# Fourth unit of a chunked RWKV6 and SiLU-MLP kernel: bonus products and a weight difference put elsewhere in the order, two quarter products exchanged

## The chip, the cores and the metric

The kernel runs on one core of one Trainium2 chip. The metric is the time on the device in microseconds (us); lower is better. Three timed runs of the kernel before gave 632.41, 632.80 and 632.97 us, median 632.8 us.

The engines are called as in the profile: PE is the matmul engine (PEld its weight loads), DVE the vector engine, ACT the scalar engine, POOL GpSimd, SP the engine that here only issues DMAs. A "q" behind a name is the engine's sequencer, where it waits for semaphores or issues DMAs.

## The reference

Two blocks follow each other. The first is a linear attention with a decay of its own for each channel (batch 4, 8 heads, 768 tokens, head size 48), the second a two-layer MLP with SiLU on the 3072 tokens (384 channels, 2048 hidden):

```python
for t in range(S):
    cur = np.einsum('bhd,bhe->bhde', u[None] * kt, vt)      # bonus of the token itself
    y[:, :, t] = np.einsum('bhd,bhde->bhe', rt, state + cur)
    state = wt[:, :, :, None] * state + np.einsum('bhd,bhe->bhde', kt, vt)
...
h = x @ w_in                                                # x: 3072 x 384
g = h * (1.0 / (1.0 + np.exp(-h)))
return (g @ w_out).astype(np.float32)
```

## The kernel before, in words

**Units.** The work is cut into 12 units, numbered 0 to 11: each is 128 tokens of two batches, 256 tokens in all. Units 0 to 2 are written out step by step together with the rounding of the weights; from unit 3, the fourth, a loop takes over. The change touches unit 3 and, in one point, every unit's output products.

**Attention of one unit.** The 128 tokens of a chunk see each other through a 128x128 matrix `score`, built in levels l = 0 to 6: at level l, blocks of 2^l tokens are paired. Before level l can be multiplied, the keys `tk` must have been grown by decays (`grow_keys`, L625, POOL, two instructions for each level, with `odd_keys`, L595, ACT, that copies the odd blocks ahead of it) and the queries `tr` too (`grow_queries`, L607, DVE). `prepare(l)` does the same and writes the grown queries into a second buffer (L737 on DVE, L739 on ACT), so that `burst(l)` can multiply levels l and l+1 one right after the other (L669, PE; first into `p_sc`, then into `p_m`). `keep_level` copies a level's result under a mask into `score` (L679, DVE). `product` (L408, POOL) makes the decays `tw` of the next level.

**The bonus.** The diagonal of `score` is a product of its own. For units below 4, `bonus(0)`, `bonus(1)` and `bonus(2)` (L428, L430, L432, all POOL) multiply r, k and u into the buffer `ruk`; `bonus_sum(0)` (L437) and `bonus_sum(1)` (L441, twice) reduce it on DVE. Both `bonus(0)` and `bonus(1)` write the first half of the same buffer, so `bonus(1)` waits for `bonus_sum(0)`. `bonus_sum(1)` ends with four small DMAs on SP (`diag<-own_sums`, L447); `bonus_spread` (L575 and L577 on ACT, L578 on DVE) and `bonus_write` (L584, DVE) put the sums on the diagonal. `load_rk` (L139) and `load_u` (L259) load the next unit's r, k, w and u for the bonus; `make_block_mask` (L478 on POOL, L480 to L483 on DVE) makes a mask that units from 4 on use.

**MLP of one unit.** `up(m)`, m = 0 to 7, multiplies `w_in` (L929, PE) into `p_h`, two buffers, which ACT turns into `gt` (L938). The output product is done with seven quarter products in place of eight (a Strassen-like scheme): `quarter(which)`, which = 0 to 6, each of 8 accumulated matmuls (L995, PE) into `p_o`, two buffers, and then one or two additions on DVE (L1004) that empty it. The products need sums of `gt` quarters, called s1 to s4 here and held in `temps` (`sums`, L977, DVE), and differences of weight quarters t1, t2, t3 in the buffer `own` (`weight_sums`, L969, DVE, 128x1536 each). `weight_sums(2)` makes t3 = b22 - b12; `weight_sums(3)` then overwrites b12.

**Order.** Within an engine, instructions run in the order in which the program writes them. `mix(i)` lists the steps of unit i in groups. Behind each group the loop puts some of the MLP steps of the two units before: `downs(i - 2)`, the seven quarters of unit i - 2, then `ups(i - 1)`, the eight ups of unit i - 1. For unit 3 the counts are

```python
room = (1, 1, 0, 2, 1, 1, 1, 1, 1, 2, 2, 1, 1, 0) if i < NPAIR else (3, 2, 2, 1, 1, 1, 2, 1, 1, 1, 0)
for group, count in zip(groups, room):
    do(*group)
    for step in steps[:count]:
```

so quarters 0 and 1 come behind groups 0 and 1, quarters 2 and 3 behind group 3, quarters 4, 5 and 6 behind groups 4, 5 and 6, then up 0 behind group 7, up 1 behind group 8, ups 2 and 3 behind group 9, and ups 4 and 5 behind group 10. `burst(1)` opens group 4, `burst(3)` group 7 and `burst(5)` group 10. On PE, unit 3 therefore reads: quarters 0 to 3, burst 1, quarters 4 to 6, burst 3, ups 0 to 3, burst 5, ups 4 to 7 with the rest of the attention between them.

## Time and profile before

| what | value |
|---|---|
| timed runs, median (lowest to highest) | 632.8 us (632.41 to 632.97) |
| the profiled execution's own time | 632.14 us |
| its span, first to last instruction | 630.4 us |
| PE busy | 621.7 us, 99% of the span |
| PEld busy | 563.5 us, 89% |
| DVE / POOL / ACT busy | 434.8 (69%) / 364.5 (58%) / 187.2 us (30%) |
| TensorE clock granted, mean over the span | 0.997 of full speed |
| unit 3 on PE, quarter 0 to the end of burst 5 | 127.53 to 167.17 us |

The span is the time from the first to the last instruction of one profiled execution; its own time, 632.14 us, is what the clock of the timed runs would show for it. The times in the trace count from the span's start. A busy PE is not PE at its peak: a matmul at half clock is busy for longer, so the granted clock has to be read beside the busy time.

### The profile page before, as it was taken

The numbers are of one execution on the slowest core, as the hardware profiler recorded it, in microseconds if no ns is written. First come the engines' busy times: TensorE is split into PE (matmuls) and PEld (weight loads), VectorE is DVE, ScalarE is ACT, GpSimd is POOL, SyncE is SP. The second block draws the span as 40 slices with busy tenths as digits, with TensorE's granted clock in tenths as the row PEclk, the third lists the DMA queues.
The fourth block names the chain that finished last, engine by engine and source line by source line (L and its number), as shares of the span: only waits on it lengthen the run. The fifth ranks groups of instructions, "written<-read, shape, count | busy, mean of one in ns | idle before, by whom it ended". The sixth has DMA issues, their size and how long they took to land.

```text
span 630.4 us, 12322 instructions
## 1 busy us (share of the span) xinstructions
PE 621.7 (99%) x4606; PEld 563.5 (89%) x4606; DVE 434.8 (69%) x749; ACT 187.2 (30%) x380; POOL 364.5 (58%) x414
## 2 busy tenths in 40 slices
PE   8999999998999999999999999999999999999997
PEld 7888876897899899899899899889989989989997
DVE  7879779898695694794595586587497586561041
ACT  6798891220320320320321221221221121120110
POOL 6998298566666567577478378368468458400000
PEclk9999999998999999999999999999999999999999
DMA  9966964443534543543543543452453212100000
GB/s 229 289 177 139 191 173 50 90 78 64 109 61 70 103 65 68 102 64 58 110 63 52 120 60 53 105 75 51 99 85 52 67 43 52 34 1 27 25 1 25
DMA packets 203067, 53.25 MB, mean 84 GB/s; under 512 B 186752, under 2 KB 194816, under 8 KB 203008
## 3 DMA queue, kind: packets, MB, share of 16 engines
q1 hardware_dynamic: 201424, 51.88, 40.8%
q10 hardware_dynamic: 1584, 0.59, 0.4%
q8 instruction: 36, 0.59, 0.4%
q14 instruction: 23, 0.19, 0.1%
HBM read 43.21 MB, written 5.24 MB: 77 GB/s over the span
## 4 chain that ended last, share of the span: by engine, by line
PE 92%; DVE 3%; POOL 2%; ACT 1%; DMA 1%; issue 1%; SPq 0%; POOLq 0%; DVEq 0%; ACTq 0%
PE p_h L929 40%; PE p_o L995 31%; PE p_sc L669 5%; PE p_m L951 3%; PE p_m L807 3%; PE p_m L669 3%; PE p_m L794 3%; PE p_m L781 1%; PE p_sc L821 1%; DMA raw<-in_r_dram 1%; POOL tk L625 1%; PE p_m L845 0%; DVE score L584 0%; DVE tr L607 0%; POOL w_in_sb L241 0%
## 5 line engine op out<-in xcount | busy, mean ns | idle before, releaser
L929 PE MATMUL p_h<-xt,w_in_sb 128*128 128x256 f32 x1152 | 259.0, 382 | 0.7 <-POOL tk L649 0.7
L929 PEld LDWEIGHTS p_h<-xt,w_in_sb 128*128 128x128 f32 x1152 | 216.6, 191 | 33.0 <-POOL tk L649 0.9
L938 ACT ACTIVATE gt<-p_h 128x512 f32<-128x512 f32 x90 | 53.7, 597 | 266.2 <-PE p_h L929 266.1
L625 POOL TENSOR_TENSOR tk<-tk,tw 128x256 f32<-128x256 f32 x128 | 87.3, 702 | 71.9 <-ACT tk L595 41.2
L995 PE MATMUL p_o<-own,temps 128*128 128x192 f32 x528 | 88.1, 326 | 0.4 <-DVE temps L1004 0.4
L995 PE MATMUL p_o<-w_out_sb,gt 128*128 128x192 f32 x508 | 87.4, 328 | 0.0
L995 PEld LDWEIGHTS p_o<-own,temps 128*128 128x128 f32 x528 | 86.0, 190 | 0.8 <-DVE temps L1004 0.7
L995 PEld LDWEIGHTS p_o<-w_out_sb,gt 128*128 128x128 f32 x508 | 82.7, 190 | 0.9 <-issue 0.4
L487 POOL TENSOR_TENSOR ruk<-tokens_rk 128x768 f32<-128x768 f32 (+1 forms) x32 | 51.4, 1616 | 38.7 <-DMA tokens_rk<-in_k_dram 26.1
L408 POOL TENSOR_TENSOR tw<-tw 128x256 f32<-128x256 f32 (+6 forms) x83 | 44.0, 530 | 44.6 <-DVE tw L360 40.7
L977 DVE TENSOR_TENSOR temps<-gt 128x256 f32<-128x256 f32 x84 | 52.8, 629 | 19.0 <-ACT gt L938 19.0
L679 DVE COPY_PREDICATED score<-mask,p_sc 128x512 f32<-128x512 int8 x62 | 44.5, 772 | 15.3 <-PE p_sc L669 14.7
L607 DVE TENSOR_TENSOR tr<-tr,tw 128x512 f32<-128x512 f32 x61 | 47.5, 779 | 3.7 <-POOL tk L625 1.0
L595 ACT COPY tk<-tk 128x256 f32<-128x256 f32 x52 | 21.0, 403 | 81.7 <-POOL tk L625 67.8
L669 PEld LDWEIGHTS p_sc<-tr,tk 48*128 48x128 f32 x512 | 31.4, 187 | 10.3 <-issue 7.6
L669 PE MATMUL p_sc<-tr,tk 48*128 48x128 f32 x512 | 37.7, 285 | 0.6 <-POOL tk L625 0.6
L1004 DVE TENSOR_TENSOR partial<-p_o,partial 128x192 f32<-128x192 f32 x33 | 11.7, 354 | 28.4 <-PE p_o L995 28.4
L1004 DVE TENSOR_TENSOR temps<-p_o,partial 128x192 f32<-128x192 f32 x22 | 7.8, 357 | 33.2 <-PE p_o L995 22.4
L995 PE MATMUL p_o<-w_out_sb,temps 128*128 128x192 f32 x176 | 30.4, 326 | 0.0
L1004 DVE TENSOR_TENSOR ob<-p_o,partial 128x192 f32<-128x192 f32 x22 | 7.8, 357 | 32.4 <-PE p_o L995 32.4
L995 PEld LDWEIGHTS p_o<-w_out_sb,temps 128*128 128x128 f32 x176 | 28.9, 190 | 0.0
L487 POOL TENSOR_TENSOR tokens_rk<-tokens_rk,tokens_w 128x192 f32<-128x192 f32 (+1 forms) x32 | 27.5, 878 | 1.3
(170 smaller groups left out, 845.2 us busy)
## 6 DMA issues: line engine op xcount, KB each, us to landing
w_out_sb<-in_moe_w_in_dram SPq DMA_DIRECT2D x6, 768.0 KB, 7.0
w_out_sb<-in_moe_w_out_dram SPq DMA_DIRECT2D x4, 768.0 KB, 5.5
own<-in_moe_w_out_dram SPq DMA_DIRECT2D x4, 768.0 KB, 5.3
tokens_rk<-in_r_dram SPq DMA_DIRECT2D x8, 384.0 KB, 4.6
tokens_rk<-in_k_dram SPq DMA_DIRECT2D x8, 384.0 KB, 5.6
tokens_w<-in_w_dram SPq DMA_DIRECT2D x8, 384.0 KB, 6.6
xt<-yt SPq DMA_DIRECT2D x60, 48.0 KB, 2.0
raw<-in_w_dram SPq DMA_DIRECT2D x80, 32.0 KB, 2.5
```

Source lines behind the costliest of these rows:

```text
L408: engine.tensor_tensor(out=up, in0=t[:, :, 0::2], in1=t[:, :, 1::2], op=ALU.mult)
L487: mul = lambda out, one, two: nc.gpsimd.tensor_tensor(out=out, in0=one, in1=two, op=ALU.mult)
L595: nc.scalar.copy(out=keys(i, X[(l + 1) % 2] * L + c, [4 * c, blocks], [c, 2], [1, c]), in_=keys(i, NP * L + c, [4 * c, blocks], [NP * L + ...
L607: nc.vector.tensor_tensor(out=odd, in0=odd, in1=tw[i][l][:, :, 0::2][:, :, :, None].to_broadcast([128, Q, L >> (l + 1), c]), op=ALU.mult)
L625: nc.gpsimd.tensor_tensor(out=out, in0=have, in1=odd_products(i, l, b, *blocks), op=ALU.mult)
L669: nc.tensor.matmul(bass.AP(tensor=s_p.tensor, offset=s_p.offset, ap=[s_p.ap[0], [apart * L // 2, 2], [1, L // 2]]), lhsT=tk[i][rows, X[l % ...
L679: nc.vector.copy_predicated(out=dst, mask=masks[l][:, :, None].to_broadcast([128, NB, NP, ni, c]), data=sc[e].rearrange("p (b q) (i c) -> ...
L929: nc.tensor.matmul(p_h[:, a, :], lhsT=w_in_sb[:, c, f * 128:(f + 1) * 128], rhs=xt[i][:, c, :], start=(c == 0), stop=(c == KC - 1))
L938: nc.scalar.activation(out=gt[i, m], in_=p_h, func=AF.Silu)
L977: nc.vector.tensor_tensor(out=out, in0=one, in1=two, op=op)
L995: nc.tensor.matmul(p, lhsT=left(f), rhs=right[:, f, :], start=(f == 0), stop=(f == FH - 1))
L1004: nc.vector.tensor_tensor(out=to, in0=p, in1=known, op=ALU.add)
```

## The change

For unit 3, `bonus(0)` moves from group 4 to group 6, behind `prepare(3)`, which grows the keys of level 3. `bonus_sum(0)`, `bonus(1)` and `bonus(2)` move from group 5 to group 7, behind `burst(3)` and its first `keep_level`. `bonus_sum(1)`, `load_rk` and `load_u` move from group 7 to group 8, and `make_block_mask` from group 8 to group 9.

For all units, quarters 3 and 4 change places: quarter 3 is now s1 times t1, quarter 4 is s3 times t3. The additions behind them follow: quarter 3 has one, quarter 4 two, as before.

`weight_sums(2)`, which makes t3, moves from the end of the steps written out for unit 2 into group 2 of unit 3, behind `prepare_keys(1)`. `weight_sums(3)` keeps its place, right behind `burst(1)` in group 4.

No instruction is added or removed on any engine. On PE and ACT the order of instructions is the same as before, but for the operands of the two exchanged quarters; on SP too. On POOL and DVE the moved steps stand elsewhere.

```diff
-                      [(burst, i, 1), (keep_level, i, 1), (bonus, i, 0)],
-                      [(keep_level, i, 2), (go_on, i, 2), (bonus_sum, i, 0), (bonus, i, 1), (bonus, i, 2)],
-                      [(prepare, i, 3), (reverse_v, i)],
-                      [(burst, i, 3), (keep_level, i, 3), (bonus_sum, i, 1), (load_rk, i + 1), (load_u,)],
-                      [(keep_level, i, 4), (go_on, i, 4), (make_block_mask,)],
-                      [(prepare, i, 5), (bonus_spread, i), (bonus_write, i)],
+                      [(burst, i, 1), (keep_level, i, 1)],
+                      [(keep_level, i, 2), (go_on, i, 2)],
+                      [(prepare, i, 3), (reverse_v, i), (bonus, i, 0)],
+                      [(burst, i, 3), (keep_level, i, 3), (bonus_sum, i, 0), (bonus, i, 1), (bonus, i, 2)],
+                      [(keep_level, i, 4), (go_on, i, 4), (bonus_sum, i, 1), (load_rk, i + 1), (load_u,)],
+                      [(prepare, i, 5), (make_block_mask,), (bonus_spread, i), (bonus_write, i)],
...
-        left, right = ((g(0, 0), b11), (g(0, 1), b21), (s(1), t2), (s(2), t3), (s(0), t1), (g(1, 1), b12), (s(3), b22))[which]
+        left, right = ((g(0, 0), b11), (g(0, 1), b21), (s(1), t2), (s(0), t1), (s(2), t3), (g(1, 1), b12), (s(3), b22))[which]
...
-        for to, known in ((), ((c11, u1),), ((u2, u1),), ((u3, u2),), ((c22, u3), (u4, u2)), ((c21, u3),), ((c12, u4),))[which]:
+        for to, known in ((), ((c11, u1),), ((u2, u1),), ((u4, u2),), ((u3, u2), (c22, u4)), ((c21, u3),), ((c12, u4),))[which]:
...
-       (load_values, 3), *both(turn_k, 2), (weight_sums, 2), (up, 1, 7), (sums, 1, 2))
+       (load_values, 3), *both(turn_k, 2), (up, 1, 7), (sums, 1, 2))
...
         if i == NTOK + 1:
 
+            groups[2].append((weight_sums, 2))
             groups[4].insert(1, (weight_sums, 3))
```

## The prediction

> **What bounds the kernel now.** I read the busy shares and the chain of waits first, then the timeline of PE around unit 3, then what PE waited for there, and last the granted clock of that stretch. The page says that PE is the bound:

> ```profile
> PE 621.7 (99%) x4606; PEld 563.5 (89%) x4606; DVE 434.8 (69%) x749; ACT 187.2 (30%) x380; POOL 364.5 (58%) x414
> ...
> PE 92%; DVE 3%; POOL 2%; ACT 1%; DMA 1%; issue 1%; SPq 0%; POOLq 0%; DVEq 0%; ACTq 0%
> ```

> Only what PE idles, or does at less than full clock, can be won. The timeline of PE (start, duration, instruction, in brackets the idle time ahead and its releaser) shows unit 3 and then the same stage of unit 4:

> ```profile
> 132.83 2.76 PE L995 MATMUL p_o<-own,temps 128*128 128x192 f32 x16
> 135.98 2.87 PE L995 MATMUL p_o<-own,temps 128*128 128x192 f32 x16 [0.38 <-DVE temps L1004]
> ...
> 148.77 1.16 PE L669 MATMUL p_sc<-tr,tk 48*128 48x128 f32 x16
> 151.92 1.86 PE L669 MATMUL p_m<-tr,tk 48*128 48x128 f32 x16 [1.98 <-POOL tk L625]
> 153.71 11.55 PE L929 MATMUL p_h<-xt,w_in_sb 128*128 128x256 f32 x48
> ...
> 201.39 1.16 PE L669 MATMUL p_sc<-tr,tk 48*128 48x128 f32 x16
> 202.38 1.06 PE L669 MATMUL p_m<-tr,tk 48*128 48x128 f32 x16
> 203.38 13.22 PE L929 MATMUL p_h<-xt,w_in_sb 128*128 128x256 f32 x60
> ```

> In unit 4 the two halves of a burst start 0.99 apart; in unit 3 the second half of burst 3 starts 3.15 after the first, held by keys from POOL. POOL's own timeline says why:

> ```profile
> 146.64 1.81 POOL L430 TENSOR_TENSOR ruk<-tokens_rk 128x768 f32<-128x768 f32 x1 [1.31 <-DVE own_sums L437]
> 148.53 2.14 POOL L432 TENSOR_TENSOR ruk<-ruk,u_bc 128x768 f32<-128x768 f32 x1
> 150.63 2.52 POOL L625 TENSOR_TENSOR tk<-tk,tw 128x256 f32<-128x256 f32 x4
> ```

> The keys of level 3 (the first two of the four L625) stand behind both bonus products. The chain of waits passes just there, DVE's L437 to L430 to L432 to L625 to PE. Last, the table of stretches (length, busy of PE, PEld, DVE, ACT, POOL, then the granted clock, DMA share and rate):

> ```profile
> 150.00:152.00 2.00, 0.08 (x2) 0.09 (x2) 2.00 (x4) 0.00 (x0) 1.92 (x4) 1.00 0.48 55
> 152.00:154.00 2.00, 2.00 (x17) 1.78 (x18) 0.37 (x2) 0.00 (x0) 1.42 (x3) 0.55 0.60 153
> 154.00:156.00 2.00, 2.00 (x6) 1.61 (x6) 1.94 (x5) 0.00 (x0) 0.00 (x0) 0.60 0.27 82
> 156.00:158.00 2.00, 2.00 (x11) 1.74 (x11) 1.08 (x3) 0.47 (x1) 0.00 (x0) 1.00 0.32 40
> ```

> PE counts as fully busy from 152 to 156, at 0.55 and 0.60 of its clock. The idle time is paid twice.

> [...]2.00 x 0.45 + 2.00 x 0.40 = 1.70 us lost, so 3.4 us at half rate[...] L969 took 2.58 us at 124.45 beside POOL's L826 and 1.75 at best.

> **The change, part by part.**

> *Bonus products behind the keys.* I compare with unit 4. There quarters 2 to 4 start at 188.30 and quarter 5 at 196.10, so 2.60 a quarter; a half burst is 0.99 to 1.00; five ups take 216.52 - 203.38 = 13.14, so 2.63 an up. Unit 3 from quarter 0 (127.53) to burst 5 (165.19) has 7 quarters, 2 bursts and 4 ups: 18.39 (quarter 0 to burst in unit 4: 201.39 - 182.99 = 18.40) + 4 x 0.995 + 4 x 2.63 = 32.9 us, against 37.66 spent. The excess is 4.76 us. It splits into: the wait at 151.92, due at 149.77, 2.15; the half clock, 0.79 in that half burst (1.79 for 1.00) and 0.97 in the ups (11.48 for 10.51), 1.76; quarter 3, due at 132.83 + 2.60 = 135.43 and started at 135.98, 0.55; the restart behind it 0.2 and quarter 4 0.1.

> With the change, POOL's queue is: six L408 (end 143.08 at the latest, as L428 no longer follows), two L625 of level 2 (1.24 to 1.30) to 144.4, ACT's copy L595 (0.41) to 144.8, two L625 of level 3 (1.24) to 146.1. PE reaches the second half of burst 3 at about 148.9. The margin is 2.8 us, so the wait goes. L737, the other input, stands behind quarter 5's L1004 at 145.85 and takes 0.97 (as at 136.83) to 2.26 (as it did beside L430): 146.8 to 148.1, still early. Worth 2.15 + 1.76 = 3.9 us.

> *What the bonus now delays.* L437 must follow two L679 of burst 3's first half (its end 149.1 + 1.3 + 0.55 = 150.95). POOL: L430 1.81 to 152.8, L432 1.82 to 2.14 to 155.0; DVE: L441 1.0 to 156.0. Behind L432 on POOL stand level 4's and 5's keys (2 x 1.24, to 157.5, plus the mask's iota, 0.3); burst 5 needs them at 160.4, 37.66 - 32.9 earlier than before. Behind L441 on SP stand the four L447 (2.45, so 156.1 to 158.5, before 153.34), then three L139, two L259, 32 raw loads, five for values, and ten L857 of xt. All go 2.5 us later while PE runs 4.5 earlier. SP had waited 2.7 us for yt at L857, so L857 falls 4.3 us late against PE: last issue 189.3 + 4.3, landing 2.0, 195.6 on PE's old scale; its reader, up 0 of unit 3, starts at 203.38. Hidden. ACT's L575 and L577 wait for L447 (landing 1.8 us) until about 160.2 and end at 161.1; behind them in ACT's queue stands L938 of up 2, whose matmuls end at 157.8. It frees `p_h` at 161.7; PE wants it for up 4 at 162.4. Margin 0.7: covered, narrowly. POOL's next bonus (L487) waits for L139 to land (4.2 to 6.2 us), runs from about 164 to 170; POOL's step behind it waits for DVE's transposes of unit 4 (L360, at 176.1 before, so 171.6 with the gain). Hidden.

> *Weight difference and exchanged quarters.* L969 leaves 124.45, behind which stood eight L977, L835, six transposes, then quarter 1's L1004 at 135.56, which held quarter 3. They come earlier by 1.75[...] to 2.58. L1004 then starts at 133.8 or before, ends by 134.2, and quarter 3 starts when due: 0.55 + 0.2 + 0.1. Nothing is added to PE: quarter 3 has one L1004 and quarter 4 two, as before, in all units; I take that at zero (both orders empty `p_o` within 0.7 us, and the buffer is needed 2.6 us later). L969's new place costs DVE 1.75 to 2.58 between L607 and L737: 134.2 + 0.9 + 1.75 to 2.58 + 0.97 = 137.8 to 138.7, and burst 1's second half wants L737's queries at 135.43 + 2.60 + 1.0 = 139.0. Covered by 0.3 to 1.2 us. t3 is ready by 137.7, quarter 4 starts at 140.0.

> *Sum.* 4.76 at most. I take off 0.25 for lateness on DVE in unit 4, an estimate: L977 there now meets L487. Gain 4.5: the profiled execution's 632.14 (span 630.4) would become 627.6. The median stands 0.66 above it; the same gain from 632.8 gives **628.3 us**.

> **The rivals.**

> *Half clock only in the profile (0.24).* [...] the timed runs may idle 2 us without losing their clock. [...] Against: the profiled execution, with the loss, is the fastest of the four. Then only the idle time and quarter 3 are won, 4.5 - 1.76 = 2.75, so about 630.0. A small new wait in unit 4 of that size ends there too.

> *The wait moves (0.08).* L969 at 2.58, L737 at 2.26 beside POOL and no gain ahead of it: 135.9 + 0.9 + 2.58 + 2.26 = 141.6, 2.6 after burst 1 wants it, and a fresh 1.7 us of half clock. 4.5 - 2.6 - 1.7 = 0.2: 632.6, no change.

> *Slower (0.06): ACT held by the diagonal.* If L441 ends later than 156.7, L577 holds L938 and up 4 waits, microsecond for microsecond[...]. It must be 3 us or more late (3 + 1.7 = 4.7) to end slower, by which both bonus products would take 7 us in place of 3.9; at 5 us late, 632.8 - 4.5 + 5 + 1.7 = 635.0. Against: nothing in the trace made L430 or L432 take over 2.3.

> That the change does not do what it says is excluded as far as order goes: it moves POOL's products as described.

> **How the numbers follow.** A measurement here tells about 0.2%, 1.3 us, from no change. Main case 0.62 (gain 4.0 to 5.0, so 627.8 to 628.8), half clock or a small new wait 0.24 (629.5 to 630.5), wait moved 0.08, slower 0.06. Faster is the first two and a little of the third, 0.87; same 0.07; slower 0.06. The range leaves out the last two cases and the ends: 627.4 to 630.6.

> **What would show it.** In the profile after, right: burst 3's halves 1.0 apart; no clock below 1.00 between 150 and 160; quarter 3 2.6 after quarter 2; four ups in 10.5; burst 5 near 160.4. Wrong: PE waiting for L737 at 139, for ACT's L938 at up 4, for L1004 in unit 4's quarter 3, or for L625 again.

## The result, and the profile after

The changed kernel takes **628.4 us** (median of 6 runs, 627.84 to 628.78), the kernel before, timed with it, 632.88 us (6 runs, 632.32 to 633.98): a ratio of 0.9927, with a 95% interval of 0.9914 to 0.994, so 4.5 us less. The profiled execution took 628.39 us, its span is 626.6 us.

The timeline of PE in the changed kernel (start, duration, instruction; no idle time is noted on any of these lines) answers to the one shown of before:

```profile
133.54 5.36 PE L995 MATMUL p_o<-own,temps 128*128 128x192 f32 x32
138.84 1.18 PE L669 MATMUL p_sc<-tr,tk 48*128 48x128 f32 x16
...
148.83 1.16 PE L669 MATMUL p_sc<-tr,tk 48*128 48x128 f32 x16
149.83 1.06 PE L669 MATMUL p_m<-tr,tk 48*128 48x128 f32 x16
150.82 10.63 PE L929 MATMUL p_h<-xt,w_in_sb 128*128 128x256 f32 x48
161.38 1.16 PE L669 MATMUL p_sc<-tr,tk 48*128 48x128 f32 x16
```

The halves of burst 3 start 1.00 apart (3.15 before). Quarters 2 and 3 are now one row, as nothing parts them, and four ups take 10.56 us (11.48 before). From quarter 0 (128.24) to burst 5 PE needs 33.14 us, 37.66 before. The stretches of that time (length, busy PE, PEld, DVE, ACT, POOL, then the clock, DMA share and rate) show the clock whole:

```profile
150.00:152.00 2.00, 2.00 (x21) 1.75 (x20) 1.98 (x4) 0.00 (x0) 0.15 (x1) 1.00 0.44 49
152.00:154.00 2.00, 2.00 (x11) 1.76 (x10) 2.00 (x3) 0.29 (x1) 1.92 (x2) 1.00 0.45 57
154.00:156.00 2.00, 2.00 (x11) 1.77 (x10) 0.30 (x2) 0.60 (x2) 2.00 (x2) 1.00 0.53 191
```

The timeline of all engines shows how POOL's queue and what hangs on the bonus stand now:

```profile
143.21 2.62 POOL L625 TENSOR_TENSOR tk<-tk,tw 128x256 f32<-128x256 f32 x4
...
151.85 1.82 POOL L430 TENSOR_TENSOR ruk<-tokens_rk 128x768 f32<-128x768 f32 x1 [4.62 <-DVE own_sums L437]
...
153.75 2.14 POOL L432 TENSOR_TENSOR ruk<-ruk,u_bc 128x768 f32<-128x768 f32 x1
...
155.93 1.01 DVE L441 TENSOR_REDUCE own_sums<-ruk 128x8 f32<-128x384 f32 x2 [1.70 <-POOL ruk L432]
...
160.15 0.84 ACT L577 COPY both_b<-diag 32x16 f32<-32x16 f32 x4 [1.04 <-DMA diag<-own_sums]
...
160.90 1.18 ACT L938 ACTIVATE gt<-p_h 128x512 f32<-128x512 f32 x2
```

The keys of levels 2 and 3 are done by 145.8, 4.0 us ahead of the burst half that needs them. The two L938 in one row are those of ups 2 and 3: the first had waited behind L577 for the diagonal's DMA. From 115 to 240 us the trace shows no wait of PE.

The two spans differ by only 3.8 us. The rest lies ahead of the change: in this execution unit 3's quarter 0 begins at 128.24, in that of before at 127.53. In the other profiles below it begins between 127.45 and 128.40, whatever the edit. From burst 5 to the end both take 465.2 us (630.4 - 165.19 and 626.6 - 161.38). So the stage is compared from quarter 0 on, and the whole by the timed runs.

### The profile page after: what moved, and what is told of

Same layout as the page of the kernel before. It is cut to its first block, busy times and chain, and to the rows that moved or that the text cites. A ratio compares the mean times of both kernels' runs of the same rounds, so it can differ in the third digit from the quotient of the medians.

```text
span 626.6 us, 12324 instructions
## 1 busy us (share of the span) xinstructions
PE 620.3 (99%) x4606; PEld 562.8 (90%) x4606; DVE 438.6 (70%) x749; ACT 187.4 (30%) x380; POOL 363.7 (58%) x414
## 4 chain that ended last, share of the span: by engine, by line
PE 94%; POOL 1%; DVE 1%; ACT 1%; DMA 1%; issue 1%; POOLq 0%; ACTq 0%
PE p_h L929 41%; PE p_o L995 32%; PE p_sc L669 5%; PE p_m L951 3%; PE p_m L807 3%; PE p_m L794 3%; PE p_m L669 3%; PE p_m L781 1%; PE p_sc L821 1%; DMA raw<-in_k_dram 1%; PE p_m L372 1%; POOL tk L625 1%; PE p_m L845 0%; DVE score L584 0%; POOL w_in_sb L241 0%
## 5 line engine op out<-in xcount | busy, mean ns | idle before, releaser
L929 PE MATMUL p_h<-xt,w_in_sb 128*128 128x256 f32 x1152 | 258.1, 382 | 0.7 <-POOL tk L649 0.7
L929 PEld LDWEIGHTS p_h<-xt,w_in_sb 128*128 128x128 f32 x1152 | 215.9, 190 | 32.6 <-POOL tk L649 0.9
L938 ACT ACTIVATE gt<-p_h 128x512 f32<-128x512 f32 x90 | 53.7, 597 | 256.1 <-PE p_h L929 255.9
L625 POOL TENSOR_TENSOR tk<-tk,tw 128x256 f32<-128x256 f32 x128 | 88.7, 714 | 62.4 <-ACT tk L595 34.7
L995 PE MATMUL p_o<-own,temps 128*128 128x192 f32 x528 | 87.9, 326 | 0.0
L995 PE MATMUL p_o<-w_out_sb,gt 128*128 128x192 f32 x508 | 87.3, 328 | 0.0
L995 PEld LDWEIGHTS p_o<-own,temps 128*128 128x128 f32 x528 | 86.0, 190 | 0.2
L995 PEld LDWEIGHTS p_o<-w_out_sb,gt 128*128 128x128 f32 x508 | 82.7, 190 | 0.9 <-issue 0.4
L487 POOL TENSOR_TENSOR ruk<-tokens_rk 128x768 f32<-128x768 f32 (+1 forms) x32 | 48.5, 1527 | 46.3 <-DMA tokens_rk<-in_k_dram 33.7
L977 DVE TENSOR_TENSOR temps<-gt 128x256 f32<-128x256 f32 x84 | 55.4, 660 | 18.3 <-ACT gt L938 18.3
L408 POOL TENSOR_TENSOR tw<-tw 128x256 f32<-128x256 f32 (+6 forms) x83 | 43.8, 528 | 40.2 <-DVE tw L360 36.3
L679 DVE COPY_PREDICATED score<-mask,p_sc 128x512 f32<-128x512 int8 x62 | 44.5, 772 | 13.4 <-PE p_sc L669 12.7
L607 DVE TENSOR_TENSOR tr<-tr,tw 128x512 f32<-128x512 f32 x61 | 49.6, 813 | 3.7 <-POOL tk L625 1.1
L595 ACT COPY tk<-tk 128x256 f32<-128x256 f32 x52 | 20.9, 403 | 85.4 <-POOL tk L625 67.1
L1004 DVE TENSOR_TENSOR partial<-p_o,partial 128x192 f32<-128x192 f32 x33 | 11.8, 358 | 47.2 <-PE p_o L995 47.1
L669 PEld LDWEIGHTS p_sc<-tr,tk 48*128 48x128 f32 x512 | 31.4, 187 | 10.3 <-issue 7.3
L669 PE MATMUL p_sc<-tr,tk 48*128 48x128 f32 x512 | 37.7, 285 | 0.7 <-POOL tk L625 0.6
L1004 DVE TENSOR_TENSOR temps<-p_o,partial 128x192 f32<-128x192 f32 x22 | 7.9, 358 | 33.3 <-PE p_o L995 23.1
L995 PE MATMUL p_o<-w_out_sb,temps 128*128 128x192 f32 x176 | 30.4, 326 | 0.0
L995 PEld LDWEIGHTS p_o<-w_out_sb,temps 128*128 128x128 f32 x176 | 28.9, 190 | 0.0
L487 POOL TENSOR_TENSOR tokens_rk<-tokens_rk,tokens_w 128x192 f32<-128x192 f32 (+1 forms) x32 | 26.8, 857 | 1.3
L977 DVE TENSOR_TENSOR temps<-temps,gt 128x256 f32<-128x256 f32 x43 | 25.7, 598 | 1.5
```

Of the source, the lines that this page charges most:

```text
L408: engine.tensor_tensor(out=up, in0=t[:, :, 0::2], in1=t[:, :, 1::2], op=ALU.mult)
L487: mul = lambda out, one, two: nc.gpsimd.tensor_tensor(out=out, in0=one, in1=two, op=ALU.mult)
L595: nc.scalar.copy(out=keys(i, X[(l + 1) % 2] * L + c, [4 * c, blocks], [c, 2], [1, c]), in_=keys(i, NP * L + c, [4 * c, blocks], [NP * L + ...
L607: nc.vector.tensor_tensor(out=odd, in0=odd, in1=tw[i][l][:, :, 0::2][:, :, :, None].to_broadcast([128, Q, L >> (l + 1), c]), op=ALU.mult)
L625: nc.gpsimd.tensor_tensor(out=out, in0=have, in1=odd_products(i, l, b, *blocks), op=ALU.mult)
L669: nc.tensor.matmul(bass.AP(tensor=s_p.tensor, offset=s_p.offset, ap=[s_p.ap[0], [apart * L // 2, 2], [1, L // 2]]), lhsT=tk[i][rows, X[l % ...
```

## The experiments

Every timed run lists its mean granted clock, and these lie in groups. The stretch at half clock in the trace of before lost 1.70 us, which makes a mean of 0.997 over 630 us; a second like it would make 0.995, an estimate from that one. The table sorts the runs by it; the idle time is that of PE at the place in question, in the one profiled execution of each kernel, and what it was in the other runs is not on record. Clocks of 0.999 and 1.0 are taken together: a mean that rounds to 0.999 has lost less than 1 us of 630, too little for a stretch of 1.70. A run "halved" below is one at 0.997 or 0.995.

Runs e1 to e4 were timed on one chip together with 35 runs of the kernel before, e5 to e8 on another with 43. Each is compared with the runs of its own chip; where e5 and e6 are set beside the changed kernel, and the changed kernel beside e1, the runs come from different sessions.

| kernel | idle of PE, us | runs | clock 0.999 to 1.0 | clock 0.997 | clock 0.995 | median, us |
|---|---|---|---|---|---|---|
| before, beside e1 to e4 | 1.98 | 35 | 5 | 26 | 4 | 632.69 |
| before, beside e5 to e8 | 1.98 | 43 | 8 | 31 | 4 | 632.68 |
| changed | none | 6 | 6 | 0 | 0 | 628.40 |
| e1, bonus alone | none in burst 3 | 6 | 6 | 0 | 0 | 628.75 |
| e2, weights alone | 2.14 | 14 | 0 | 9 | 5 | 632.65 |
| e3, exchange alone | 1.98 | 14 | 6 | 8 | 0 | 632.51 |
| e4, gap filled | none | 14 | 14 | 0 | 0 | 630.98 |
| e7, half filled | 0.98 | 14 | 14 | 0 | 0 | 631.13 |
| e8, quarter filled | 1.41 | 22 | 10 | 12 | 0 | 632.16 |
| e5, less moved | none | 6 | 6 | 0 | 0 | 628.32 |
| e6, late diagonal | 2.75 | 14 | 0 | 13 | 1 | 633.17 |

The kernel before by itself has a mean of 630.93 us at clock 1.0 and of 632.70 at 0.997 in the first session, of 630.95 and 632.73 in the second: 1.77 and 1.78 us apart.

**e1: the bonus steps alone.** The group list of the change; the quarters and `weight_sums(2)` as before.

```diff
-                      [(keep_level, i, 2), (go_on, i, 2), (bonus_sum, i, 0), (bonus, i, 1), (bonus, i, 2)],
+                      [(keep_level, i, 2), (go_on, i, 2)],
...
+                      [(burst, i, 3), (keep_level, i, 3), (bonus_sum, i, 0), (bonus, i, 1), (bonus, i, 2)],
```

> Only the bonus steps of unit 3 move; the quarters keep their order and the weight difference t3 its place. Theory (burst 3's wait for level 3's keys, 2.15 us, and the half clock after it, 1.76 us, are what the bonus move removes): 632.9 - 3.9 = 629.0 us; in the profile the halves of burst 3 are 1.0 apart, no stretch below clock 1.00, but quarter 3 still starts 3.15 after quarter 2. Rival A (the half clock belongs to the profiled execution alone): 632.9 - 2.15 = 630.7 us. Rival B (the gain comes from DVE being freed of the weight difference): 632 to 633 us.

Measured: 628.75 us, ratio 0.9944 (0.9929 to 0.9959), 3.9 us less. Its timeline of PE:

```profile
132.75 2.76 PE L995 MATMUL p_o<-own,temps 128*128 128x192 f32 x16
135.88 2.87 PE L995 MATMUL p_o<-own,temps 128*128 128x192 f32 x16 [0.36 <-DVE temps L1004]
...
148.68 1.16 PE L669 MATMUL p_sc<-tr,tk 48*128 48x128 f32 x16
149.67 1.06 PE L669 MATMUL p_m<-tr,tk 48*128 48x128 f32 x16
```

Burst 3 no longer waits, and quarter 3 still does, 3.13 after quarter 2. Quarter 0 to burst 5 takes 33.77 us, 3.89 less than before. Almost the whole gain is this part. Both rivals fall.

**e2: the weight difference and the exchange, without the bonus steps.** The two lines of the exchange are those of the change and are left out here.

```diff
-       (load_values, 3), *both(turn_k, 2), (weight_sums, 2), (up, 1, 7), (sums, 1, 2))
+       (load_values, 3), *both(turn_k, 2), (up, 1, 7), (sums, 1, 2))
...
+            groups[2].append((weight_sums, 2))
```

> Only the weight difference t3 moves and the two quarters are exchanged; the bonus steps stay. Theory: quarter 3's wait of 0.55 and its 0.2 to 0.3 of restart go, burst 3's wait for the keys and the half clock stay; the chain to those keys hangs on quarter 4, so it comes earlier with it: 632.9 - 0.8 = 632.1 us. Rival A: the keys do not come earlier, burst 3 waits 0.8 longer: 632.9 us, no change. Rival B (DVE is what counts): 629 to 630 us.

Measured: 632.65 us, ratio 1.0007 (0.9997 to 1.0017): no difference in the median. The theory's 0.8 is missed. Its timeline of PE says where it went:

```profile
138.67 1.18 PE L669 MATMUL p_sc<-tr,tk 48*128 48x128 f32 x16
...
148.67 1.16 PE L669 MATMUL p_sc<-tr,tk 48*128 48x128 f32 x16
151.97 1.16 PE L669 MATMUL p_m<-tr,tk 48*128 48x128 f32 x16 [2.14 <-POOL tk L625]
```

Counted from its quarter 0 (128.08), PE reaches burst 1 after 10.59 us (11.25 before), so the part does win 0.66 there. At burst 3 PE comes 0.65 earlier, but the keys only 0.50, so the wait grows from 1.98 to 2.14. What is left shows in the runs at clock 0.997: their mean is 632.27, 0.43 below that of before. But no run kept its clock whole (5 of 35 before did), and 5 of 14 are at 0.995, against 4 of 35 before. In the median the two cancel; with 14 runs, chance may have a part in these shares. The keys did come earlier, but not by as much as the theory had it, so the result lies between the theory and rival A.

**e3: the exchange of the quarters alone.** The additions behind the two quarters follow, as in the change.

```diff
-        left, right = (..., (s(1), t2), (s(2), t3), (s(0), t1), (g(1, 1), b12), (s(3), b22))[which]
+        left, right = (..., (s(1), t2), (s(0), t1), (s(2), t3), (g(1, 1), b12), (s(3), b22))[which]
```

> Only quarters 3 and 4 are exchanged, in all units; t3 and the bonus stay. Theory: no change, within 0.3 us of 632.9. Rival (u3, made in quarter 4 now, or the later c22 holds p_o or the output): 0.1 us in each of 12 units, 634 us.

Measured: 632.51 us, ratio 0.9992 (0.9981 to 1.0003). At clock 0.997 its mean is 632.88 and at 1.0 it is 630.97, against 632.70 and 630.93. No change, as the theory had it: the exchange only lets t3 be made later. Its gap before the keys is the 1.98 us of before, but only 8 of its 14 runs halved, against 30 of 35; such shares are rough with so few runs.

**e4: the gap filled with work.** The kernel before, with PE kept busy where it waits for the keys:

```diff
         score_products(i, l, before.pop((i, l)), made[i, l])
+        if (i, l) == (3, 3):
+            p = ps.tile([128, L], F32, name="p_h", bufs=2)
+            for x in range(16):
+                nc.tensor.transpose(p, ident, ident)
```

> The kernel before, with 16 transposes of the identity on PE between the two halves of unit 3's burst 3, into a p_h buffer that is free there: at the 0.11 us of a transpose in the trace (8 in 1.04 less overlap) they fill 1.8 of the 2.0 us in which PE waits for the keys. The wait itself stays. Theory (the half clock follows from that idle time, in the timed runs too): no stretch below clock 1.00, and 632.9 - 1.7 = 631.2 us. Rival A (the timed runs have no half clock): 632.9 us. Rival B (the clock falls for another reason than the idle time): profile still shows 0.55 and 0.60, 632.9 to 633.1 us.

Measured: 630.98 us, ratio 0.9973 (0.9965 to 0.9981), 1.7 us less with 16 transposes more. Its timeline of PE and its table of stretches (the new lines shift the later line numbers by four):

```profile
148.98 1.16 PE L669 MATMUL p_sc<-tr,tk 48*128 48x128 f32 x16
150.07 1.97 PE L752 MATMUL p_h<-ident 128*128 128x128 f32 x16
152.15 1.16 PE L669 MATMUL p_m<-tr,tk 48*128 48x128 f32 x16
153.24 10.63 PE L933 MATMUL p_h<-xt,w_in_sb 128*128 128x256 f32 x48
```

```profile
152.00:154.00 2.00, 1.89 (x21) 1.66 (x21) 1.04 (x3) 0.00 (x0) 1.57 (x4) 1.00 0.52 113
154.00:156.00 2.00, 2.00 (x11) 1.77 (x10) 1.86 (x7) 0.00 (x0) 0.00 (x0) 1.00 0.38 126
```

The wait is as long as ever (the halves start 3.17 apart), and the ups behind it take 10.55 in place of 11.48. This shows that the half clock follows from PE's idle time. The timed runs say the same: the mean of e4 at clock 1.0, 630.89, is that of the kernel before in its five runs at 1.0, 630.93, and the other 30 are slower, the 26 at 0.997 by 1.77 us and the 4 at 0.995 by 2.82. Rival A, the first rival of the prediction, falls for these 30 and holds for the five.

**e7 and e8: the gap filled in part.** As e4 with 8 and with 4 transposes.

> As e4, but 8 transposes in place of 16, so that about 1.1 us of idle time of PE are left in the gap. Theory ([...]less idle time means fewer halvings): most runs at clock 1.0, near 630.9 us, few or none at 632.7. Rival (any wait of this kind halves the clock): as the kernel before, 632.7 us with a clock of 0.997.

> As e4, but 4 transposes, so that about 1.5 us of idle time are left. Theory: a mixture, some runs at clock 1.0 and 630.9 us, some at 0.997 and 632.7, fewer halved than the 30 of 35 of the kernel before. Rival: as the kernel before.

Measured: e7 631.13 us, ratio 0.9974 (0.9962 to 0.9986), e8 632.16 us, ratio 0.9985 (0.9974 to 0.9996). The timelines of PE of the two, in this order:

```profile
152.79 1.16 PE L669 MATMUL p_m<-tr,tk 48*128 48x128 f32 x16 [0.98 <-POOL tk L625]
```

```profile
152.03 1.16 PE L669 MATMUL p_m<-tr,tk 48*128 48x128 f32 x16 [1.41 <-POOL tk L625]
```

With 0.98 us of idle time left none of 14 runs halved, with 1.41 us 12 of 22 did, with 1.98 us 35 of 43. The profiled execution of e8 was one of the unhalved. So the rival falls: not every wait of this kind halves the clock, and with less idle time fewer runs halved. At a given length it comes in some runs and not in others, and nothing on record tells which. That 1.41 us is safer than 1.98 is likely, but rests on few runs: e3, with 1.98 us, halved as seldom as e8.

**e5: less moved.** The changed kernel, with product 0, both sums and the loads back where the kernel before has them, so that of the bonus only products 1 and 2 move. The mask stays where the change puts it, unlike what the expectation says:

```diff
+                      [(burst, i, 1), (keep_level, i, 1), (bonus, i, 0)],
+                      [(keep_level, i, 2), (go_on, i, 2), (bonus_sum, i, 0)],
+                      [(prepare, i, 3), (reverse_v, i), (bonus, i, 1), (bonus, i, 2)],
+                      [(burst, i, 3), (keep_level, i, 3), (bonus_sum, i, 1), (load_rk, i + 1), (load_u,)],
+                      [(keep_level, i, 4), (go_on, i, 4)],
```

> The changed kernel, but of the bonus only products 1 and 2 move, to right behind the keys of level 3; product 0, both sums, the loads and the mask stay where the kernel before has them. Theory (what counts is that the keys of level 3 stand ahead of products 1 and 2 on POOL; all else was covered): the same as the changed kernel, 628.1 to 628.7 us; the diagonal's DMAs leave some 3 us earlier and win nothing. Rival (their lateness in the changed kernel cost something in unit 4): 628.0 us or less. Rival B (product 0 ahead of level 2's keys delays those of level 3): 629 to 631 us, PE waiting for L625 again.

Measured: 628.32 us (627.78 to 630.01), ratio 0.9923 (0.9903 to 0.9944), not to be told from the changed kernel; quarter 0 to burst 5 takes 33.20 us (33.14 there). The order on POOL was what counted; the lateness of the diagonal cost nothing that these runs can show. No version here beats the changed kernel.

**e6: the slower rival put to the test.** The changed kernel with product 1 done three times, which leaves the same result:

```diff
-                      [(burst, i, 3), (keep_level, i, 3), (bonus_sum, i, 0), (bonus, i, 1), (bonus, i, 2)],
+                      [(burst, i, 3), (keep_level, i, 3), (bonus_sum, i, 0), *[(bonus, i, 1)] * 3, (bonus, i, 2)],
```

> The changed kernel with bonus product 1 of unit 3 done three times in place of once (the same result again), so that product 2, L441 and the diagonal's DMAs come 3.6 us later. Theory (ACT's queue is held by L577, behind it stands up 2's L938, and up 4 needs its buffer): in the changed kernel L938 of up 2 ended at 161.5 and up 4 started at 163.36, so the margin is 1.9; 3.6 to 4.0 later PE waits 1.7 to 2.1 us ahead of up 4, and the clock halves in most runs, 1.8 more: 628.4 + 1.7 = 630.1 us to 632.3 us. Rival (keys of levels 5 and 6, which stand behind product 2 on POOL, are late first): PE waits for L625 at burst 5, over 2 us. Rival B (ACT is not held): 628.4 us.

Measured: 633.17 us, ratio to the kernel before 1.0004 (0.9992 to 1.0016), 4.8 above the changed kernel. Its timeline of all engines:

```profile
159.35 1.01 DVE L441 TENSOR_REDUCE own_sums<-ruk 128x8 f32<-128x384 f32 x2 [5.47 <-POOL ruk L432]
...
164.68 0.84 ACT L577 COPY both_b<-diag 32x16 f32<-32x16 f32 x4 [2.15 <-DMA diag<-own_sums]
...
165.42 1.06 ACT L938 ACTIVATE gt<-p_h 128x512 f32<-128x512 f32 x2
...
166.06 9.72 PE L929 MATMUL p_h<-xt,w_in_sb 128*128 128x256 f32 x36 [2.75 <-ACT gt L938]
```

The mechanism is as the theory had it: the diagonal's DMAs, 4.0 KB each, hold ACT (2.15 us of idle time ahead of L577), ACT holds `p_h`, and up 4 waits. Its size was set too low: 2.75 us of idle time where 1.7 to 2.1 was expected. L441 came 3.42 later by the clock of the trace, 3.76 counted from quarter 0 of each, and the last of L447's DMAs landed later after its issue (L577 began 2.3 after the issues ended at 162.38; in the changed kernel 1.2, 160.15 after 158.96); why it did is open. The rival of late keys falls: burst 5's halves start 1.11 apart, 0.99 in the changed kernel. With a half clock in all 14 runs that is 2.75 + 1.78 = 4.53 of the 4.8.

## Why the prediction was right, point by point

- **Burst 3's wait**, put at 2.15. At clock 1.0 the kernel before takes 630.93 and e1 628.83 (5 runs of each): 2.10. Right. The keys' margin, put at 2.8, is 4.0 (145.8 to 149.83); L737's queries, the other input, ended at 147.8, 2.0 ahead.
- **The half clock**, put at 1.76. Between the two groups of the kernel before lie 1.77 and 1.78 us, and e4 shows its cause. The likeliest case took it for certain in the timed runs; it was in 65 of 78. The rival was right that a run can wait 2 us and keep its clock, as 13 of 78 did, and against such a run the change wins only 2.5 us (630.95 - 628.41). The six runs of before in the result, none below 632.3, look like halved ones, so 4.5 was measured.
- **Quarter 3's wait**, put at 0.85 (0.55, and 0.3 of "restart" behind it). From quarter 0 to burst 1 the changed kernel takes 10.60, before 11.25: 0.65. This term was too large: only the wait itself and 0.1 went. Quarter 4 (2.71 before) takes 2.70 still (140.84 to 143.54), and quarters 2 and 3 take 5.30 together, not 5.20. What I had called a restart is mostly not one; what it is, no run here shows. In the timed runs at clock 1.0, e1 (628.83) against the changed kernel (628.41), the part is worth some 0.4 us, as in e2 at clock 0.997.
- **DVE's lateness in unit 4**, put at 0.25. It did not come, though L977 did meet L487 (one took 2.03 us at 168.23, the two behind it 1.21 and 1.24; those of before, from 170.99 to 174.43, 0.42 to 0.43 each): quarter 0 to burst 3 takes 18.45 us there (179.18 to 197.63), 18.40 before, and with the same 465.2 us from burst 5 to the end nothing that the prediction called hidden came to light later. The two errors, 0.2 and 0.25, went opposite ways, so that 4.5 was met by the sum (37.66 - 33.14 = 4.52) better than by its terms. That they cancelled is luck.
- **L969's new place** cost DVE 2.21, within the 1.75 to 2.58 given; L737 behind it ended at 138.94 and burst 1's second half began at 139.85, undelayed. Behind its old place quarter 1's L1004 came 1.79 earlier (6.24 after quarter 0, 8.03 before), near the low end of the same range. That end was an estimate from L969's shortest time; why L969 takes 1.75 in one place and 2.58 in another, no run here isolates.
- **ACT held by the diagonal**: margin put at 0.7, it is 1.9 (L938 of up 2 ended at 161.5, up 4 began at 163.36). L441 ended at 156.94, put at 156.0, of which 0.7 is the later start of the whole stage in this execution. Even so up 4 did not wait, though 156.7 had been named as the limit: the diagonal's last DMA landed 1.2 us after its issue ended, put at 1.8, the four issues ended 2.0 after L441, put at 2.5, and PE came to up 4 some 0.25 later in its stage than reckoned. e6 shows that the rival was real: 3.76 us of lateness and 1.1 more for the landing, less the margin of 1.9, make 3.0, and the wait was 2.75.

## What to carry to other kernels

POOL ran its queue in the order of the program: in the kernel before the keys of level 3 began at 150.63, behind L432, and in the changed kernel they were done by 145.8, ahead of L428 and L430. On such an engine, look for work that nobody waits for soon ahead of work that the bottleneck waits for next; moving two POOL products of 1.8 to 2.1 us behind two key products was worth 0.6% here. Read the granted clock behind the waits of the matmul engine: here one of 1.98 us was in 65 of 78 runs paid again as half clock (1.77 to 1.78 us), and where it could not be removed, filling it with matmuls that nobody needs won that second part back (e4, 1.7 us less), even when half of it was filled (e7, 1.55 us less). And before a step is put later, walk along everything that stands behind its results in other queues, as e6's 3.8 us of lateness turned a gain of 4.5 into nothing.

## What the runs showed of the hardware

Some runs have a mean clock of 0.995 (8 of 78 at 1.98 us, 5 of 14 at 2.14 us). A second such stretch would explain it, an estimate from the 1.70 us above; no profile here caught one, and these runs are slower than those at 0.997 by amounts from 0.9 us (e6) to 2.1 us (before, second session). So when two runs of one kernel lie some 2 us apart, that need not be noise: in the kernel before the runs at clock 1.0 and at 0.997 lie 1.77 to 1.78 us apart.
